# Half differences and sums as two chains with one-bank PSUM tiles, and a bank add on VectorE: a gated mix of two attention branches

## The chip, the cores and the metric

The kernel runs on one core of a Trainium2 chip, in one launch. The metric is the device time of an execution in microseconds (us). TensorE (PE) multiplies matrices, VectorE (DVE), ScalarE (ACT) and GpSimd (POOL) work elementwise, SyncE (SP) issues most transfers. Of these GpSimd reads and writes SBUF only; matmuls land in PSUM, eight banks of 128 x 512 fp32.

## What is computed

Two attention branches on the same input of 2048 positions and 512 features, 32 heads of 16, mixed by a gate for each position (cut to what matters):

```python
g = sigmoid((x * gate_w).sum(-1, keepdims=True))
# A: each position sees itself and 7 earlier ones, 2 apart
qkv = x @ wqkv
logits = einsum("bhsd,bhswd->bhsw", q, kg) * scale      # masked where idx < 0
a = (einsum over w of softmax(logits), vg) @ wo_a
# B: all 2048 positions; 32 query heads share one key head and one value head
scores = einsum("bhqd,bkd->bhqk", x @ wq, x @ wk) * scale
b = (softmax(scores) @ (x @ wv)) @ wo_b
return g * a + (1 - g) * b
```

Branch B needs 32 x 2048 x 2048 scores twice here: once for the maximum over the keys of each query, which is subtracted before the exponential, and once for the exponential itself.

## The kernel before

**Units and steps.** Branch B is cut into 32 units (512 queries by 4 heads). A unit's queries lie stacked in one of eight SBUF tiles (`qst`, the last two of them `q67`), two heads in each 64-row half, so that a matmul over 64 rows runs in one row half of TensorE and another beside it in the other. The attention loop has 512 steps, 16 to a unit (128 keys each): two `exp_pair` (L503; scores of two heads into `eb[0]` or `eb[1]`, two banks each, and ScalarE's exponential of 128 x 1024, L510) and one `weighted` (L515; eight recorded matmuls of the step before into `po`, L518).

**Maxima.** The maximum of a unit must be known before its first step. `slots` lists the work: 1024 entries (unit, pair, 128 queries, 512 keys), two matmuls each, one to a row half. They run ahead of the loop and beside it, in three ways:
- `fill_pair` (L373): two matmuls (`max_mm`, L351) into the two banks of `m2` (`pm` in the profile), and one VectorE maximum over both (L378).
- `fill_one` (L382): one matmul into `m1` (`ps`), or `po` where that is free, and a VectorE maximum (L389). In a loop step it stands alone in its row half.
- the half path, for two key blocks at once, since max(a, b) = (a + b) / 2 + |a - b| / 2. `kcd` holds the half sums and half differences of the keys (`half_keys`, L410). `fill_diff` (L445): two matmuls with the half differences into both banks of `m2` (L443), an Abs by ScalarE on each bank into `dd` (L453). `fill_sum` (L458): a matmul with the half sums into `m1` or `po`, then one VectorE instruction adds `dd` and takes the maximum (L463). Four matmuls as in the plain way, but 2 x 512 columns for VectorE in place of 4 x 512.

Before, one such group of four is open at a time: `pend` holds its two sums, and `fill_diff` runs only when `pend` is empty and both banks of `m2` are free (L783).

**Stages.** First the projection: queries, keys, values of B, then 48 row parts of branch A's projection (`lumps` of kind `a`: three column thirds of 16 row parts), each 12 products split over both row halves (L1124) into `eb`. `a_post` (L260) ends such a part: ScalarE copies both banks out (L274, L275), GpSimd adds them (L281), SP stores. GpSimd then computes branch A's attention in the background (`work`, L1012). The loop is interrupted twice, before step 272 and before step 400, by output phases (`out_phase`, L792; eight and four row blocks of the final projections, L804). The last four output row blocks are spread over the last steps (`spread`, L840, and `spread_some`, L899; L872), once no fills are left, on blocks that `blocks_out` (L711) turns by DMA from step 472 on. If the fills are late, `pause` (L925) stops the loop for them.

**Order.** All instructions are written out by a planner in program order: `clk` estimates the time at which TensorE, ScalarE and VectorE are done, `free` when a PSUM bank can be written again, and work is placed when these say that it is ready. In the projection and the output phases `stream` (L753) does it: it keeps a place in the list of products for each row half, puts a sum or a single in one half and a product in the other, and a pair in a slot of its own. A queue runs in order, so a matmul that must wait holds all behind it. In the loop the main code (L1177 on) asks `fill_ready` (L915) for a pair between the two `exp_pair`, and for a single while `singles` (L911) says that more matmuls are left than the pairs of the remaining steps can take.

## Time and profile before

| what | value |
|---|---|
| median of 3 runs | 1477.92 us (1476.96 to 1478.03) |
| the profiled execution | 1477.72 us, of it the span 1475.9 us |
| granted TensorE clock, mean | 0.997 |
| busy share of the span | PE 99%, DVE 82%, ACT 86%, POOL 69% |
| projection with half groups, 105 to 258 us | ScalarE 127.18 of 153 us, VectorE 104.76 |
| first loop part, from about 258 us | 272 steps |
| first output phase, 836 to 908 us | then 128 steps |
| second output phase, 1175 to 1211 us | then 112 steps |
| tail, 1381 to 1464 us | TensorE 78.97 of 83 us, mean clock 0.96 |

A row of the timeline gives start (us), duration (us), engine, line, operation, written and read tiles, form and count; equal neighbours are merged. Matmuls overlap, so the distance from one start to the next tells more than a duration. In brackets stand the idle time ahead of a row and what ended it. `pe` is `eb`, `pm` is `m2`, `ps` is `m1`, and 62*128 or 64*128 tells rows and columns of the array in use.

### The profile page before, as it was taken

The page shows a single profiled execution, that of the slowest core. Times are in us where ns is not written, and L with a number is a line of the kernel's source. Part 1 is how long each engine was busy: PE and PEld are TensorE (multiplying, and loading weights), DVE is VectorE, ACT ScalarE, POOL GpSimd, SP SyncE. Part 2 cuts the span into 40 slices and gives each one's busy share as a digit, 9 for nine tenths or more (in the row PEclk, how much of TensorE's full clock was granted, in tenths as well). Part 3 has the DMA queues.
Part 4 walks back from the last instruction along what each step waited for, and adds up shares of the span by engine and source line. Part 5 has one row for each costly group of instructions (what it writes and reads, how often), then busy time and mean ns, then how long its engine had stood idle before and what let it go on. Part 6 is the DMA issues. An engine that isn't in the chain of part 4 may idle for free.

```text
span 1475.9 us, 28719 instructions
## 1 busy us (share of the span) xinstructions
PE 1462.1 (99%) x10612; PEld 681.4 (46%) x10612; DVE 1210.2 (82%) x1851; ACT 1269.2 (86%) x1592; POOL 1023.9 (69%) x1772
## 2 busy tenths in 40 slices
PE   9999999999999999999999999999999999999998
PEld 5878787333333333333333475333333363333343
DVE  6976667789898898888898888888888888888922
ACT  5668788999999999999999878999999889999865
POOL 7854988878988989989889898788888231110121
PEclk9999999999999999999999999999999999999999
DMA  6753524121120211211202111121120000000110
GB/s 223 211 161 91 143 72 119 39 85 41 56 70 27 74 60 42 71 40 50 75 7 76 42 67 53 41 71 41 42 70 23 12 31 12 2 1 8 23 30 29
DMA packets 75260, 89.77 MB, mean 61 GB/s; under 512 B 56368, under 2 KB 56416, under 8 KB 70896
## 3 DMA queue, kind: packets, MB, share of 16 engines
q1 hardware_dynamic: 68176, 49.00, 11.7%
q0 software_dynamic: 6368, 37.90, 7.8%
q8 instruction: 83, 1.36, 0.4%
q10 hardware_dynamic: 576, 1.05, 0.2%
q14 instruction: 57, 0.47, 0.1%
HBM read 60.03 MB, written 27.35 MB: 59 GB/s over the span
## 4 chain that ended last, share of the span: by engine, by line
PE 87%; DVE 1%; ACT 1%; SPq 1%; issue 0%; DMA 0%; DVEq 0%; ACTq 0%; POOL 0%
PE po L518 34%; PE pe L508 23%; PE pm L351 8%; PE ps L351 7%; PE pe L1124 5%; PE pe L804 4%; PE pm L443 2%; PE ps L443 1%; PE po L443 1%; PE pm L872 1%; SPq L728 0%; DVE mx L378 0%; PE pe L693 0%; ACT pexp L453 0%; DMA td<-raw 0%
## 5 line engine op out<-in xcount | busy, mean ns | idle before, releaser
L510 ACT ACTIVATE pexp<-pe 128x1024 f32<-128x1024 f32 x1022 | 990.4, 1022 | 105.1 <-PE pe L508 102.1
L378 DVE TENSOR_REDUCE mx<-pm 128x2 f32<-128x1024 f32 x500 | 611.8, 1224 | 117.7 <-PE pm L351 114.8
L518 PE MATMUL po<-pexp,vst 128*32 128x512 f32 x4096 | 546.8, 606 | 0.1
L508 PE MATMUL pe<-qst,kst 64*128 64x512 f32 x1916 | 435.2, 448 | 2.8 <-DVE mx L378 1.8
L508 PEld LDWEIGHTS pe<-qst,kst 64*128 64x128 f32 x1916 | 180.0, 184 | 477.5 <-ACT pexp L510 462.4
L389 DVE TENSOR_REDUCE mx<-ps 128x1 f32<-128x512 f32 x494 | 336.1, 680 | 4.5 <-PE ps L351 4.5
L351 PE MATMUL pm<-kst,qst 62*128 62x512 f32 x942 | 192.2, 396 | 0.9 <-DVE mx L378 0.9
L582 POOL TENSOR_TENSOR pr<-aext 128x256 f32<-128x256 f32 x256 | 182.2, 737 | 0.3
L351 PE MATMUL ps<-kst,qst 62*128 62x512 f32 x459 | 181.9, 396 | 0.4 <-DVE mx L463 0.2
L642 POOL TENSOR_TENSOR oa<-oa,av 128x256 f32<-128x256 f32 x224 | 164.1, 732 | 15.4
L518 PEld LDWEIGHTS po<-pexp,vst 128*32 128x32 f32 x4096 | 80.6, 108 | 180.1 <-issue 171.6
L639 POOL TENSOR_TENSOR av<-aext,lg 128x256 f32<-128x256 f32 x224 | 139.3, 622 | 12.9
L453 ACT ACTIVATE dd<-pm 128x512 f32<-128x512 f32 x150 | 85.0, 609 | 24.3 <-PE pm L443 21.2
L545 POOL TENSOR_TENSOR rl<-rl,gate_t 128x16 f32<-128x16 f32 x31 | 6.9, 222 | 131.0 <-DVE rl L539 97.1
L1124 PE MATMUL pe<-wal,xh 64*128 64x512 f32 x376 | 94.4, 392 | 0.2 <-POOL wal L84 0.2
L1124 PE MATMUL pe<-wah,xh 64*128 64x512 f32 x376 | 93.8, 392 | 0.1
L351 PEld LDWEIGHTS pm<-kst,qst 62*128 62x128 f32 x942 | 92.0, 187 | 3.7 <-DVE mx L378 1.6
L1124 PE MATMUL pe<-wah,xl 64*128 64x512 f32 x376 | 92.9, 392 | 0.0
L463 DVE CUSTOM_DVE_ANT_0 dd<-ps,dd 128x512 f32<-128x512 f32 x75 | 51.9, 692 | 48.3 <-PE ps L443 39.9
L351 PEld LDWEIGHTS ps<-kst,qst 62*128 62x128 f32 x459 | 85.8, 187 | 6.6 <-DVE mx L389 2.4
L588 POOL TENSOR_TENSOR tr<-pr 128x512 f32<-128x512 f32 x64 | 81.7, 1277 | 4.2
L281 POOL TENSOR_TENSOR stage<-stage,two 128x512 f32<-128x512 f32 x48 | 62.5, 1302 | 23.1 <-ACT two L275 22.6
(217 smaller groups left out, 1825.2 us busy)
## 6 DMA issues: line engine op xcount, KB each, us to landing
aext<-ad POOLq DMA_DIRECT2D x32, 1056.0 KB, 5.6
qst<-qd SPq DMA_DIRECT2D x60, 128.0 KB
ad<-stage SPq DMA_DIRECT2D x32, 240.0 KB
xraw<-xt SPq DMA_DIRECT2D x16, 256.0 KB
qd<-qhi SPq DMA_DIRECT2D x16, 256.0 KB
qd<-qlo SPq DMA_DIRECT2D x16, 256.0 KB
qst<-qd SPq DMA_DIRECT2D x60, 64.0 KB
qst<-ml SPq DMA_DIRECT2D x216, 2.0 KB
```

Source lines behind the costliest of these rows:

```text
L351: nc.tensor.matmul(dst, qst[home(v)[0]][b:b + 62, pr, t * P:(t + 1) * P], kst[b:b + 62, kc * 512:(kc + 1) * 512], start=True, stop=True)
L378: nc.vector.tensor_reduce(m[:, :, pr, t, kc], dst, AX.X, ALU.max)
L389: nc.vector.tensor_reduce(m[:, odd, pr, t, kc:kc + 1], dst, AX.X, ALU.max)
L453: nc.scalar.activation(dd[0][:, odd], m2[:, odd, :], AF.Abs)
L508: nc.tensor.matmul(bank[:, odd, :], kst[b:b + 64, kt * P:(kt + 1) * P], qst[home(u)[0]][b:b + 64, pr, :], start=True, stop=True)
L510: nc.scalar.activation(e, bank, AF.Exp, scale=SCALE)
L518: nc.tensor.matmul(po[32 * i:32 * i + 32, :], vst[:, kt, :], pexp[s, i // 2][:, i % 2, :], start=(kt == 0), stop=(kt == NJ - 1))
L582: nc.gpsimd.tensor_mul(pr[:, k], q, e[:, o:o + NH, AC:2 * AC])
L588: nc.gpsimd.tensor_add(nx, cur[:, :, 0:n], cur[:, :, n:2 * n])
L639: nc.gpsimd.tensor_mul(av, e[:, o:o + NH, 2 * AC:].rearrange("p j (h d) -> p j h d", d=DH), lg[:, w].unsqueeze(3).to_broadcast([P, NH, AG, ...
L642: nc.gpsimd.tensor_add(ao, ao, av)
L1124: nc.tensor.matmul(front[2 if x == last else x % 2][0][:, b, :], l[h], r[h], start=(i == 0), stop=(i == 3 * C - 1))
```

## The change

1. **Two chains.** `fill_diff` and `fill_sum` take a row half. `groups` holds groups of which a difference is still to be issued, `pend` the sums that wait, one list for each half, and `half_free` when each bank of `m2` is free. `diff_ready` and `sum_ready` decide for each half, so that in one slot `stream` may place a sum or a difference in one half and a product, or the other half's chain, in the other. `dd` has two buffers in the projection instead of one. At the end of a stream the rest is issued in the same way.
2. **One-bank tiles.** The class `Banks` makes `m2` either one tile of two banks (plain pairs, scores, output rows) or two tiles of one bank each (half path), so that instructions on one bank do not wait for the other's.
3. **Row parts.** For every third row part (j % 3 == 0, but for the first of all; 17 of 48) ScalarE copies one bank only, and VectorE adds the second from PSUM to it. GpSimd's add goes away there.
4. The two tiles that form the half keys' selector share the buffers of tag `aext`.

The core of the diff:

```diff
+class Banks:
+    def shape(self, n):
+        if len(self.tiles) != n:
+            if self.pool:
+                self.pool.release()
+            self.pool = self.tc.alloc_tile_pool(name=self.name + "s", bufs=1, space=PSUM)
+            if n == 1:
+                self.tiles = [self.pool.tile([P, 2, 512], F32, name=self.name)]
+            else:
+                self.tiles = [self.pool.tile([P, 512], F32, name=self.name, tag=f"{self.name}{b}") for b in range(2)]
+        return self
...
-            two = (p2 if j % 3 else pm)[0].tile([P, GN], F32, name="two", tag=("two", "raw", "own")[j % 3], bufs=1)
+            two = p2[0].tile([P, GN], F32, name="two", tag=("", "raw", "own")[j % 3], bufs=1) if j % 3 else None
         own = st[:, j % 2, :]
         nc.scalar.activation(own, bank[:, 0, :], AF.Copy)
-        nc.scalar.activation(two, bank[:, 1, :], AF.Copy)
-        at = after("act", clk["pe"] + T_LAT, 1.05)
+        if two:
+            nc.scalar.activation(two, bank[:, 1, :], AF.Copy)
+        at = after("act", clk["pe"] + T_LAT, 1.05 if two else 0.52)
...
-            nc.gpsimd.tensor_add(own, own, two)
-            pool = max(pool, 1e3 * at) + 1280
+            if two:
+                nc.gpsimd.tensor_add(own, own, two)
+                pool = max(pool, 1e3 * at) + 1280
+            else:
+                nc.vector.tensor_add(own, bank[:, 1, :], own)
+                free[key] = after("dve", at, 0.65) + 0.1
...
-    def fill_diff():
-        v, pr, t, kc = slots.pop(0)
-        slots.pop(0)
-        for odd in range(2):
-            half_mm(m2[:, odd, :], v, pr, t, kc, 1, odd)
...
+    def diff_ready(odd):
+        if max(half_free) != free["m2"]:
+            half_free[:] = [free["m2"]] * 2
+        if half_free[odd] > clk["pe"] or clk["dve"] - 1.6 > clk["pe"]:
+            return False
+        mine = [g for g in groups if odd in g[2]]
+        if not mine and (groups or half or ended or wants or not paired()):
+            return False
+        d = mine[0][1] if mine else dd[0]
+        return all(x[1] is not d for x in pend[odd])
+
+    def fill_diff(odd):
...
+        m2.shape(2)
+        half_mm(m2[:, odd, :], v, pr, t, kc, 1, odd)
+        nc.scalar.activation(d[:, odd], m2[:, odd, :], AF.Abs)
+        half_free[odd] = after("act", clk["pe"] + T_R + T_LAT, 0.54) + 0.1
+        free["m2"] = max(half_free)
+        pend[odd].append(((v, pr, t, kc), d, half_free[odd]))
...
+    def sum_ready(odd):
+        return bool(pend[odd]) and free[("m1", "po")[odd]] <= clk["pe"] + 0.1 and pend[odd][0][2] <= clk["pe"] + 0.4
...
             halves = groups or any(pend) or paired() and not half
             if halves or 1 in wants:
                 for b in range(2):
                     if sum_ready(b):
                         lone[b] = lambda b=b: fill_sum(b)
                     elif diff_ready(b):
                         lone[b] = lambda b=b: fill_diff(b)
                         break
```

Where the program's rows move. First TensorE in the projection, within one of the last row parts (unit 7 of the maxima, `pm` the differences, `ps` and `po` the sums of the two halves). Before:

```order
L443 MATMUL pm<-kcd,qst_82 128x512 x2
L1124 MATMUL pe_85<-wah,xh 128x512 x2
L1124 MATMUL pe_85<-wal,xh 128x512 x2
L443 MATMUL ps<-kcd,qst_82 128x512
L1124 MATMUL pe_85<-wah,xl 128x512 x2
L1124 MATMUL pe_85<-wah,xh 128x512 x2
L1124 MATMUL pe_85<-wal,xh 128x512
L443 MATMUL po<-kcd,qst_82 128x512
L1124 MATMUL pe_85<-wal,xh 128x512
```

In the change, in the same row part:

```order
L480 MATMUL ps<-kcd,q_76 128x512
L1185 MATMUL pe_85<-wal,xh 128x512 x2
L1185 MATMUL pe_85<-wah,xl 128x512
L480 MATMUL pm<-kcd,q_76 128x512
L1185 MATMUL pe_85<-wah,xh 128x512
L480 MATMUL po<-kcd,q_76 128x512
L1185 MATMUL pe_85<-wah,xl 128x512
L480 MATMUL pm<-kcd,q_76 128x512
L1185 MATMUL pe_85<-wah,xh 128x512
```

The pair of differences in a slot of its own has become two single differences, each beside a product or beside the other half's sum, and there are more of them to a row part; over the whole projection 372 half matmuls stand where 300 stood (164 for 140 and 76 for 68 in the output phases).

Second TensorE in the loop at steps 421 and 422 (`ps` the single, L518 or L578 the weighted sum that ends a step). Before:

```order
L508 MATMUL pe_85<-qst_77,kst 128x512 x2
L351 MATMUL pm<-kst,qst_79 128x512 x2
L508 MATMUL pe_86<-qst_77,kst 128x512 x2
L351 MATMUL ps<-kst,qst_79 128x512
L518 MATMUL po<-pexp,vst 32x512 x4
```

In the change, step 421 still with its single and step 422 without:

```order
L384 MATMUL pm<-kst,qst_81 128x512 x2
L568 MATMUL pe_86<-qst_77,kst 128x512 x2
L384 MATMUL ps<-kst,qst_81 128x512
L578 MATMUL po<-pexp,vst 32x512 x4
L568 MATMUL pe_85<-qst_77,kst 128x512 x2
L384 MATMUL pm<-kst,qst_81 128x512 x2
L568 MATMUL pe_86<-qst_77,kst 128x512 x2
L578 MATMUL po<-pexp,vst 32x512 x4
```

From step 422 to 479 the single is gone; before, each step up to 487 has it.

Third TensorE at steps 479 and 480, where in the change the output rows begin (L933). Before, step 480:

```order
L508 MATMUL pe_85<-qst_81,kst 128x512 x2
L351 MATMUL pm<-kst,qst_82 128x512 x2
L508 MATMUL pe_86<-qst_81,kst 128x512 x2
L351 MATMUL ps<-kst,qst_82 128x512
L518 MATMUL po<-pexp,vst 32x512 x4
```

In the change, step 479 and the beginning of step 480:

```order
L384 MATMUL pm<-kst,qst_82 128x512 x2
L568 MATMUL pe_86<-qst_81,kst 128x512 x2
L578 MATMUL po<-pexp,vst 32x512 x4
L568 MATMUL pe_85<-qst_81,kst 128x512 x2
L933 MATMUL pm<-woh_3672,turned_15661 128x512 x6
L568 MATMUL pe_86<-qst_81,kst 128x512 x2
L578 MATMUL po<-pexp,vst 32x512 x4
```

The output rows start at step 480 instead of step 490, and the five pairs on `pe` and `pm` that a pause put ahead of the scores of step 488 are gone.

More of the change, by code (lines that the diff above doesn't have):

```diff
@@ L373, in fill_pair @@
     def fill_pair(dst, key):
+        if dst is m2:
+            dst = m2.whole()
         v, pr, t, kc = slots.pop(0)
@@ L503, in exp_pair @@
     def exp_pair(s, pr, other=False, first=0):
-        bank, key = (m2, "m2") if other else (eb[pr], f"e{pr}")
+        bank, key = (m2.whole(), "m2") if other else (eb[pr], f"e{pr}")
         u, kt = divmod(s, NJ)
@@ L766, in stream @@
+            if halves or 1 in wants:
+                for b in range(2):
+                    if sum_ready(b):
+                        lone[b] = lambda b=b: fill_sum(b)
+                    elif diff_ready(b):
+                        lone[b] = lambda b=b: fill_diff(b)
+                        break
             elif fillable() and free["m1"] <= clk["pe"] + 0.1:
-                single, odd = lambda: fill_one(m1, "m1"), half[0][4] if half else 0
+                lone[half[0][4] if half else 0] = lambda: fill_one(m1, "m1")
@@ L775, in stream @@
                     clk["pe"] = now
                 elif at[b] < len(seq):
[L777 removed]
+                    dur = max(dur, mm(b, seq[at[b]]))
                     at[b] += 1
[L779 to L785 removed]
+            after("pe", 0, T_R if lone else dur)
@@ L786, in stream @@
+            if not (ended or 0 in wants or halves) and slots and fillable() and free["m2"] <= clk["pe"] + 0.1:
                 clk["pe"] = max(clk["pe"], free["m2"])
@@ L831, in out_phase @@
         stream([(x, j, i) for x, j in enumerate(js) for i in range(m)], mm, done, False)
-        while pend:
-            odd = pend[0][4]
-            clk["pe"] = max(clk["pe"], free[("m1", "po")[odd]], ready_d[odd] - 0.3)
-            fill_sum()
+        ended.add(1)
+        while groups or any(pend):
+            for b in range(2):
+                if sum_ready(b):
+                    fill_sum(b)
+                elif diff_ready(b):
+                    fill_diff(b)
             clk["pe"] += T_R
@@ L1163, in gated_mix_kernel @@
     stream([(x, i) for x in range(len(lumps)) for i in range(3 * C)], mm, done_mm, True)
-    assert not pend
+    assert not groups and not any(pend)
     formed.clear()
```

81 lines of the change are left out of this document (43 added, 38 removed).

## Prediction

> **What bounds the kernel now.** I read the page first (span, chain), then busy time by stage, then single steps of the attention loop in order of time, then the tail.
>
> ```profile
> span 1475.9 us, 28719 instructions
> PE 87%; DVE 1%; ACT 1%; SPq 1%; issue 0%; DMA 0%; DVEq 0%; ACTq 0%; POOL 0%
> ```
>
> The chain that ended last is TensorE for 87% of the span. The profiled execution took 1477.72 us (1.8 us outside its span), 0.2 us below the median of 1477.92, so sums against it need no correction. By stage (projection before and from its first half groups on, first output phase, last steps):
>
> ```profile
> core 0: us, PE busy (x) PEld busy (x) DVE busy (x) ACT busy (x) POOL busy (x), PEclk, DMA share, GB/s
> 24.00:105.00 81.00, 79.98 (x641) 64.18 (x641) 70.57 (x99) 51.24 (x109) 64.81 (x57) 1.00 0.63 175
> 105.00:258.00 153.00, 152.38 (x1256) 121.58 (x1256) 104.76 (x310) 127.18 (x255) 117.92 (x161) 1.00 0.41 111
> 836.00:908.00 72.00, 70.99 (x615) 52.41 (x617) 57.80 (x162) 57.41 (x108) 66.33 (x103) 1.00 0.14 49
> 1381.00:1464.00 83.00, 78.97 (x564) 33.16 (x556) 31.23 (x43) 62.23 (x64) 19.23 (x35) 0.96 0.09 20
> ```
>
> TensorE is busy throughout the first three, ScalarE and VectorE are not; only the tail lets TensorE idle, at a mean clock of 0.96. Matmuls over 64 rows run two at a time, one per row half: a slot of the projection takes 153.00 / (1256 / 2) = 0.244 us, of the output phase 72.00 / (615 / 2) = 0.234 us.
>
> A full step of the attention loop (TensorE's rows, then one of ScalarE's):
>
> ```profile
> 500.14 0.50 PE L508 MATMUL pe<-q,kst 64*128 64x512 f32 x2
> 500.48 0.40 PE L351 MATMUL pm<-kst,qst 62*128 62x512 f32 x2
> 500.72 0.39 PE L508 MATMUL pe<-q,kst 64*128 64x512 f32 x2
> 500.95 0.40 PE L351 MATMUL ps<-kst,qst 62*128 62x512 f32 x1
> 501.28 1.07 PE L518 MATMUL po<-pexp,vst 128*32 128x512 f32 x8
> 502.27 0.51 PE L508 MATMUL pe<-q,kst 64*128 64x512 f32 x2
> ```
>
> ```profile
> 502.88 1.94 ACT L510 ACTIVATE pexp<-pe 128x1024 f32<-128x1024 f32 x2 [0.20 <-PE pe L508]
> ```
>
> From 500.14 to 502.27 is 2.13 us: 0.34 + 0.24 + 0.23 + 0.33 + 0.99, with no gap, while ScalarE waits 0.20 us for the next scores. A single maximum matmul (ps) costs a whole slot, 0.23 us, since nothing runs in the other half. So **TensorE's issue order bounds every stage**, and what matters is how many slots the change moves where.
>
> **The change, part by part.** The order says where the 2048 maximum matmuls stand. Half differences and sums: projection 300, now 372 (+72); first output phase 140, now 164 (+24); second 68, now 76 (+8). Plain ones: first loop 790, now 773; middle loop 370 and 372; last loop 271, now 179. So 104 matmuls leave plain fills, mostly of the last loop.
>
> *Projection.* +72 matmuls are 36 slots: 36 x 0.244 = **+8.8 us**, as TensorE has no idle time there that could hide them. Beside it ScalarE gains 36 Abs and loses 17 copies, GpSimd loses 17 adds, VectorE gains 36 reductions and 17 adds:
>
> ```profile
> L453 ACT ACTIVATE dd<-pm 128x512 f32<-128x512 f32 x148 | 83.9, 610 | 23.0 <-PE pm L443 19.9 <-DVE mx L463 2.9
> L463 DVE CUSTOM_DVE_ANT_0 dd<-ps,dd 128x512 f32<-128x512 f32 x74 | 51.2, 692 | 46.4 <-PE ps L443 38.1 <-ACT dd L453 7.2 <-PE pe L1124 0.7
> ```
>
> ```profile
> L747 DVE TENSOR_TENSOR two<-pe,two x12: 685/685/687, 848.6 to 1211.5; 128x512 f32<-128x512 f32 x12
> ```
>
> ScalarE: 83.9 / 148 = 0.57 us of its time per Abs, and a copy of the same shape costs about the same, so (36 - 17) x 0.57 = +10.8 on 127.18, in a window of about 162 us: 138 of 162. VectorE: 36 x 0.69 + 17 x 0.69 = +36.6 on 104.76 (L747 is the same add, bank plus copy): 141 of 162. Neither reaches its limit, so I cost their work at nothing; if that cover fails, TensorE waits (the drains, below). Waits also change: today a difference pair can wait for the Abs of both banks, 49 times in all:
>
> ```profile
>   PEld pm L443: 14.6, 49
> ```
>
> ```profile
> 238.97 0.50 PE L443 MATMUL pm<-kcd,qst 62*128 62x512 f32 x2
> 239.32 0.40 PE L1124 MATMUL pe<-wah,xl 64*128 64x512 f32 x2
> ```
>
> Such a slot took 0.35 us instead of 0.24, so an unmet wait costs **0.11 us** beyond what it waits. Now each bank waits alone, and the planner asks for zero slack where it took 0.1 us; but there are more waits. Bounds: all 49 vanish (-5.4), or as many again (+5.4). I take no change, the nearest count there is. Queued behind a waiting difference stands all of TensorE's stream; behind the new bank add stand VectorE's reductions, 0.69 us of delay each time, which a planner slack of up to 1.6 us covers.
>
> *First loop.* Steps 12 to 18 (seven) have no single and mostly no pair, since more of the eight stacked units are used up; the rest equals before. Before they take 6 x 2.13 + 1.90 (the last step of a unit has no single today either, below) = 14.7 us, now 7 x 2.01 (below) = 14.1: **-0.6**. The unit that the fills wait for comes in by DMA in step 17 and is first used in step 19, by the order; I cost that wait at nothing, as the planner leaves two steps for it.
>
> *Output phases.* (12 + 4) x 0.234 = **+3.7**.
>
> *Steps 422 to 479.* 58 steps lose their single. How fast is such a step? Once per unit there is one today:
>
> ```profile
> 326.09 0.50 PE L508 MATMUL pe<-qst,kst 64*128 64x512 f32 x2
> ...
> 327.99 0.50 PE L508 MATMUL pe<-qst,kst 64*128 64x512 f32 x2
> ...
> 328.71 0.49 PE L508 MATMUL pe<-qst,kst 64*128 64x512 f32 x2
> 329.14 1.06 PE L518 MATMUL po<-pexp,vst 128*32 128x512 f32 x8
> 330.13 0.51 PE L508 MATMUL pe<-qst,kst 64*128 64x512 f32 x2
> ```
>
> ```profile
> 326.72 3.81 ACT L510 ACTIVATE pexp<-pe 128x1024 f32<-128x1024 f32 x4 [0.21 <-PE pe L508]
> 330.74 1.02 ACT L510 ACTIVATE pexp<-pe 128x1024 f32<-128x1024 f32 x1 [0.21 <-PE pe L508]
> ```
>
> The step from 326.09 took 1.90 us, but in the next one ScalarE ran four exponentials back to back ((3.81 - 1.02) / 3 = 0.93 apart), and the second scores (328.71) waited for the end of the second (326.72 + 0.93 + 1.02 = 328.67). What is late next is this ring over two steps: scores to weighted sum 0.43, to next scores 0.99, to their exponential 0.61, to the second 0.93, its run 1.02, release 0.04 = 4.02 us, **2.01 us a step**. Bounds: TensorE's 1.90 below, today's 2.13 above. 58 x (2.13 - 2.01) = **-7.0** (-13.3 to 0).
>
> *Tail, steps 480 to 510.* Before:
>
> ```profile
> 1380.59 1.06 PE L518 MATMUL po<-pexp,vst 128*32 128x512 f32 x8
> ...
> 1400.80 0.51 PE L351 MATMUL pe<-kst,qst 62*128 62x512 f32 x2 [0.93 <-DVE mx L378]
> 1401.93 0.50 PE L351 MATMUL pm<-kst,qst 62*128 62x512 f32 x2 [0.62 <-DVE mx L378]
> 1404.19 1.22 PE L508 MATMUL pe<-qst,kst 64*128 64x512 f32 x4 [1.76 <-DVE mx L378]
> ...
> 1444.42 0.51 PE L508 MATMUL pe<-qst,kst 64*128 64x512 f32 x2
> ...
> 1446.78 0.51 PE L508 MATMUL pe<-qst,kst 64*128 64x512 f32 x2
> ...
> 1462.51 1.07 PE L518 MATMUL po<-pexp,vst 128*32 128x512 f32 x8
> ```
>
> From 1380.59 to 1462.51, 31 steps, are 81.9 us: fills until step 487, a pause that ends the last fills (three waits for VectorE, then half clock), then the last four output rows at three to five pairs a step, 2.36 us with three. Now the fills are over at step 479, and the same 84 row pairs spread over 480 to 510: by the order eleven steps with three pairs, twenty with two (2.36 - 0.23 = 2.13): 11 x 2.36 + 20 x 2.13 = 68.6. At each of three row changes VectorE empties the bank in two passes; I allow 0.2 us each, an estimate: 69.2, **-12.7**. Bounds: -14, or -5 if the rows wait for their inputs.
>
> By the Trainium skill ("TensorE: Matmul & The Clock Gate", Part 1) the clock halves after an idle window of some 3.4 us; the 0.96 in the tail's row agrees. By that rule a new wait of such length anywhere would cost another stretch at half clock: the sum would be 1473 (the tail's row has 83.00 x 0.04 = 3.3 us of clock lost), against 1470 without.
>
> Sum: +8.8 - 0.6 + 3.7 - 7.0 - 12.7 = -7.8; 1477.7 - 7.8 = **1470 us**.
>
> At nothing as well: the selector matrices move into buffers of the bank copies, whose third add comes before them on GpSimd, and the pair bank changes its shape between stages, where its last reader was waited for already. That the change doesn't do what it says is no rival: the order rows shown with it have its moves.
>
> **The rivals.**
> - *The drains bound the projection* (slower). In the first output phase, where the same chains run, VectorE was 57.80 / 72.00 = 80% busy and ScalarE 80% too, and the rest went in waits for each other and TensorE. If the projection's chains reach no more than that, VectorE's 141.4 us need 177 us, not 162: 1470 + 15 = 1485, seen as unmet waits of 0.11 us and more before half matmuls. It decides from 82% on (141.4 / (161.8 + 10.8)). For: VectorE goes from 68% to 87%, and 612 half matmuls now wait one by one. Against: in the projection's first part (24 to 105 us) VectorE held 87% with TensorE 99% busy. A rule speaks for it: the Trainium skill, "TensorEngine Tiling (Array Packing)", PSUM Bottleneck, says that tiling speeds up TensorE but not the emptying of PSUM, which may then become the bottleneck. By the rule the sum ends at 1485, by the row from 24 to 105 us at 1470; no row has these chains at 87%.
> - *TensorE's own 1.90 for the steps without a single* (58 x 0.11 = 6 more) *and half of the 49 waits gone* (2 to 3 more): 1462. Against: ScalarE's ring above.
> - *The rows wait.* They start ten steps earlier, on blocks turned by DMA from step 472 on; if these are late, the tail gains 5, not 12.7: 1478.
>
> **How the numbers follow.** Forecast 1470 (1465 to 1474, the bounds of the waits): 0.60. Drains, 1485: 0.17. Faster still, 1462: 0.13. Late rows, 1478: 0.10. A measurement of this kernel can tell 0.2%, 3 us. Faster by more than that (under 1475): 0.60 + 0.13 less 0.02 for the forecast's upper edge = 0.71; same: 0.10 + 0.02 = 0.12; slower: 0.17. A range to 1482 leaves out most of the drains' case and little else: 1462 to 1482.
>
> **What would show it.** Right: the loop starts about 9 us later; steps 422 to 479 at 2.01; no pause at step 488 and a clock of 1.00 there; first weighted sum of step 480 to that of 510 about 69 us. Wrong: difference matmuls of 0.50 us in the projection by the hundred, or a wait for blocks in the first steps of the tail.

## The result, and the profile after

The changed kernel takes **1475.81 us** (median of 20 runs, 1475.48 to 1476.37) against 1478.03 of the kernel before in the same session: a ratio of **0.9984, 95% interval [0.9977, 0.9991]**. It is 2.2 us faster, where 1470, 7.8 us faster, was forecast. The direction was right, the size was not: less than a third of the gain arrived.

The page of the changed kernel, span and chain of waits:

```profile
span 1474.1 us, 29007 instructions
PE 97%; DVE 1%; ACT 1%; issue 1%; POOL 0%; DMA 0%; DVEq 0%; SPq 0%; ACTq 0%; POOLq 0%
```

TensorE carries 97% of the chain now, and the tail no longer idles. Busy time by stage (projection in two parts, first output phase, steps 476 to 510):

```profile
core 0: us, PE busy (x) PEld busy (x) DVE busy (x) ACT busy (x) POOL busy (x), PEclk, DMA share, GB/s
24.00:105.00 81.00, 79.62 (x637) 64.86 (x636) 71.88 (x104) 50.80 (x109) 63.03 (x55) 1.00 0.63 174
105.00:270.00 165.00, 162.90 (x1335) 122.18 (x1333) 137.23 (x398) 139.88 (x279) 118.95 (x193) 1.00 0.38 105
848.00:922.00 74.00, 73.53 (x623) 52.22 (x619) 63.04 (x185) 61.79 (x118) 66.24 (x105) 1.00 0.17 57
1382.00:1462.00 80.00, 80.00 (x600) 31.68 (x598) 15.97 (x26) 70.94 (x74) 19.33 (x35) 1.00 0.11 23
```

The last row has TensorE busy for all of its 80 us at a clock of 1.00 (0.96 before), as forecast. In the projection VectorE is at 137.23 of 165 us, 83%, and ScalarE at 85%: close to the loads that were worked out, and still not full.

The first matmuls of the weighted sums (L578) of steps 0, 479 and 510 give the stages; step 480 begins behind the second of them:

```profile
272.45 0.64 PE L578 MATMUL po<-pexp,vst 128*32 128x512 f32 x4
...
1391.95 1.06 PE L578 MATMUL po<-pexp,vst 128*32 128x512 f32 x8
...
1460.85 1.06 PE L578 MATMUL po<-pexp,vst 128*32 128x512 f32 x8
```

| stage (start of one step's weighted sum to another's) | before | after | difference | forecast |
|---|---|---|---|---|
| projection, to step 0 | 260.62 | 272.45 | +11.8 | +8.8 |
| steps 0 to 18 | 38.99 | 37.57 | -1.4 | -0.6 |
| step 19 | 2.13 | 3.21 | +1.1 | 0 |
| first output phase (with its step) | 70.28 | 75.51 | +5.2 | +2.8 |
| second output phase | 35.71 | 37.22 | +1.5 | +0.9 |
| steps 401 and 402 | 4.49 | 5.16 | +0.7 | 0 |
| steps 422 to 479 | 123.94 | 116.67 | -7.3 | -7.0 |
| steps 480 to 510 | 81.92 | 68.90 | -13.0 | -12.7 |
| everything else | | | -0.5 | 0 |

The two large gains came within 0.3 us of the forecast. The costs did not: the stages with half matmuls took 6 us more than forecast, and single places another 1.8.

**Slots or waits?** A slot is a pair of matmuls that start together, one per row half. Counting slots between the first and the last of a stage, and taking 0.229 us for each, what is left over is time in which a slot was late:

| | slots before | left over | slots after | left over |
|---|---|---|---|---|
| projection | 967 | 14.6 us | 1003 | 18.2 us |
| first output phase | 272 | 6.0 us | 286 | 8.0 us |
| second output phase | 135 | 2.8 us | 141 | 3.0 us |

So 56 slots more, 12.8 us, where the forecast had 52 and 12.5 us; and 5.8 us more of late slots (29.2 us in place of 23.4), where it had none.

**Which slots are late.** Here is one sum in the projection of the changed kernel, on TensorE, with the one before it in the same bank (ps):

```profile
174.95 0.40 PE L480 MATMUL ps<-kcd,qst 62*128 62x512 f32 x1
...
175.90 0.39 PE L1185 MATMUL pe<-wal,xh 64*128 64x512 f32 x1
176.25 0.49 PE L480 MATMUL ps<-kcd,qst 62*128 62x512 f32 x1
...
176.60 0.39 PE L1185 MATMUL pe<-wah,xh 64*128 64x512 f32 x1
```

The weight load of the second sum, and VectorE's reduction of the first between the two:

```profile
176.25 0.18 PEld L480 LDWEIGHTS ps<-kcd,qst 62*128 62x128 f32 x1 [0.39 <-DVE mx L523]
```

```profile
175.50 0.69 DVE L523 CUSTOM_DVE_ANT_0 dd<-ps,dd 128x512 f32<-128x512 f32 x1
176.12 0.08 DVE L523 DVE_READ_ACCUMULATOR2_ANT mx<- 128x1 f32 x1
```

The sum stands five slots behind the one before it in its bank, 5 x 0.23 = 1.15 us. But the ring takes longer: matmul start to reduction 0.55, reduction 0.69 and 0.01, then 0.05 to the next matmul: 1.30 us. VectorE was not late here; it began 0.55 us behind the matmul, about as early as it ever does (over all sums of the projection, the reduction ends 1.22 us behind the matmul at best, and the next matmul of that bank starts at 1.29). So the slot ahead of the sum lasts 0.35 us instead of 0.23, and the slot behind it 0.35 as well.

The planner (L516 and L524) thinks the ring is 0.23 + 0.20 + 0.66 + 0.08 = 1.17 us and lets a sum go 0.1 us before that, at 1.07: five slots pass, and five slots are too short. In the changed kernel 38 sums of the projection, 23 of the first output phase and 11 of the second stand five slots (one of them four) behind the last in their bank; the slots next to these 72 are 12.2 us longer than 0.229 each. In the kernel before, whose one group had to finish before the next began, none of the projection's sums stands closer than six; in the output phases four do.

Two more losses are single events. On GpSimd a weight split (L112) waits behind another split and an add, and TensorE for it; and in step 19 a fill waits for unit 8's DMA:

```profile
205.76 1.29 POOL L112 TENSOR_TENSOR wal<-waraw,wah 128x512 fp32r<-128x512 f32 x1
207.00 1.30 POOL L311 TENSOR_TENSOR stage<-stage,two 128x512 f32<-128x512 f32 x1
208.25 1.27 POOL L112 TENSOR_TENSOR wal<-waraw,wah 128x512 fp32r<-128x512 f32 x1
```

```profile
209.58 0.49 PE L1185 MATMUL pe<-wal,xh 64*128 64x512 f32 x1 [1.50 <-POOL wal L112]
```

```profile
312.56 0.47 PE L384 MATMUL pm<-kst,qst 62*128 62x512 f32 x1 [0.80 <-DMA qst<-qd]
```

### The profile page after: what moved, and what is told of

Same layout as the page of the kernel before. It is cut to its first block, busy times and chain, and to the rows that moved or that the text cites. A ratio compares the mean times of both kernels' runs of the same rounds, so it can differ in the third digit from the quotient of the medians.

```text
span 1474.1 us, 29007 instructions
## 1 busy us (share of the span) xinstructions
PE 1461.2 (99%) x10612; PEld 670.5 (45%) x10612; DVE 1191.0 (81%) x1880; ACT 1289.0 (87%) x1629; POOL 1001.4 (68%) x1753
## 4 chain that ended last, share of the span: by engine, by line
PE 97%; DVE 1%; ACT 1%; issue 1%; POOL 0%; DMA 0%; DVEq 0%; SPq 0%; ACTq 0%; POOLq 0%
PE po L578 34%; PE pe L568 23%; PE pe L1185 11%; PE pm L384 8%; PE ps L384 7%; PE pe L862 5%; PE pm L480 3%; PE po L480 2%; PE ps L480 2%; PE pm L933 1%; PE pe L208 1%; ACT pexp L570 1%; DVE qst L186 0%; POOL wal L112 0%; PE pe L753 0%
## 5 line engine op out<-in xcount | busy, mean ns | idle before, releaser
L413 DVE TENSOR_REDUCE mx<-pm 128x2 f32<-128x1024 f32 x491 | 600.9, 1224 | 147.2 <-PE pm L384 136.4
L578 PE MATMUL po<-pexp,vst 128*32 128x512 f32 x4096 | 545.5, 605 | 0.0
L424 DVE TENSOR_REDUCE mx<-ps 128x1 f32<-128x512 f32 x420 | 285.7, 680 | 0.0
L384 PE MATMUL ps<-kst,qst 62*128 62x512 f32 x408 | 161.4, 396 | 0.3 <-DVE mx L424 0.2
L578 PEld LDWEIGHTS po<-pexp,vst 128*32 128x32 f32 x4096 | 80.5, 108 | 171.3 <-issue 162.6
L506 ACT ACTIVATE dd<-pm 128x512 f32<-128x512 f32 x186 | 104.9, 604 | 23.4 <-PE pm L480 13.1
L1185 PE MATMUL pe<-wal,xh 64*128 64x512 f32 x376 | 118.8, 395 | 1.9 <-POOL wal L112 1.9
L1185 PE MATMUL pe<-wah,xh 64*128 64x512 f32 x376 | 119.8, 397 | 0.0
L1185 PE MATMUL pe<-wah,xl 64*128 64x512 f32 x376 | 118.9, 395 | 0.0
L506 ACT ACTIVATE pexp<-pm 128x512 f32<-128x512 f32 x120 | 68.2, 603 | 13.7 <-PE pm L480 9.5
L384 PEld LDWEIGHTS ps<-kst,qst 62*128 62x128 f32 x408 | 76.1, 187 | 6.4 <-DVE mx L424 3.4
L648 POOL TENSOR_TENSOR tr<-tr 128x256 f32<-128x256 f32 (+1 forms) x128 | 72.4, 565 | 8.8
```

What stands on the lines that cost most here:

```text
L384: nc.tensor.matmul(dst, qst[home(v)[0]][b:b + 62, pr, t * P:(t + 1) * P], kst[b:b + 62, kc * 512:(kc + 1) * 512], start=True, stop=True)
L413: nc.vector.tensor_reduce(m[:, :, pr, t, kc], dst, AX.X, ALU.max)
L424: nc.vector.tensor_reduce(m[:, odd, pr, t, kc:kc + 1], dst, AX.X, ALU.max)
L506: nc.scalar.activation(d[:, odd], m2[:, odd, :], AF.Abs)
L578: nc.tensor.matmul(po[32 * i:32 * i + 32, :], vst[:, kt, :], pexp[s, i // 2][:, i % 2, :], start=(kt == 0), stop=(kt == NJ - 1))
L648: nc.gpsimd.tensor_add(nx, cur[:, :, 0:n], cur[:, :, n:2 * n])
```

## The experiments

The theory: the half matmuls of the chains come earlier than their banks can be free, because the planner's clock is too fast for the ring through VectorE, and each costs a late slot or two. The rivals: half matmuls cost more than half a slot by themselves, since slots stay half empty; or VectorE (or ScalarE) has no capacity left. All kernels below are the changed one with the edit shown; medians are to be read beside its 1475.81, ratios are to the kernel before, run on the same chip (1478.3 to 1478.6).

**1. Drains made short, TensorE's order kept.**

```diff
-nc.scalar.activation(d[:, odd], m2[:, odd, :], AF.Abs)
+nc.scalar.activation(d[:, odd, 0:64], m2[:, odd, 0:64], AF.Abs)
-nc.vector.tensor_tensor_reduce(d[:, odd], dst, d[:, odd], 1.0, -FMAX, ALU.add, ALU.max, m[:, odd, pr, t, kc:kc + 1])
+nc.vector.tensor_tensor_reduce(d[:, odd, 0:64], dst[:, 0:64], d[:, odd, 0:64], 1.0, -FMAX, ALU.add, ALU.max, m[:, odd, pr, t, kc:kc + 1])
```

> The Abs on ScalarE and the fused reduction on VectorE that empty the banks of the half matmuls work on 64 of the 512 columns, in the projection and in both output phases; TensorE's order is that of the changed kernel, row for row. The output's shifts are then maxima over fewer keys. Theory of waits (half matmuls wait for the drain of their bank, or work queued behind the drains comes late): in the projection the time above 0.229 us a slot, 18.9 us now, falls by 6 to 8 (all slots longer than 0.25 us before or behind a half matmul), in the output phases, 11.2 us now, by 3 to 5, so the kernel takes 1464 to 1467 us. Rival of slots (the matmuls of the two row halves no longer start together, half slots stay empty, drains have no part in it): at most the late weight split goes, 1.7 us, so 1474 to 1476 us.

Measured 1462.81 us, 0.9894 [0.9881, 0.9908]. The loop starts 7.8 us earlier, the output phases are 4.5 and 1.7 us shorter, and the rest is about 0.5 us longer:

```profile
264.61 0.64 PE L578 MATMUL po<-pexp,vst 128*32 128x512 f32 x4
```

The order of matmuls is the same, so slots stay what they are, and the rival of half-empty slots is out: **14.1 us of the changed kernel are waits for the drains**, in the output phases more than the theory allowed for (the weight split is still late here, 1.9 us at 202.2). Left over above 0.229 for each of the same slots are 10.3, 3.5 and 1.3 us, 15.1 in all. The kernel before has 23.4, so part of that may be waits for drains too; its drains were not shortened in any run.

**2. Only VectorE's reduction short.**

```diff
-nc.vector.tensor_tensor_reduce(d[:, odd], dst, d[:, odd], 1.0, -FMAX, ALU.add, ALU.max, m[:, odd, pr, t, kc:kc + 1])
+nc.vector.tensor_tensor_reduce(d[:, odd, 0:64], dst[:, 0:64], d[:, odd, 0:64], 1.0, -FMAX, ALU.add, ALU.max, m[:, odd, pr, t, kc:kc + 1])
```

> Only VectorE's fused reduction is shortened to 64 of 512 columns (it leaves 448 columns out of the maxima); the Abs on ScalarE stays whole, TensorE's order stays. Theory of waits, VectorE's part: in the projection of the changed kernel 68 of 79 waits of half matmuls' weight loads end with VectorE, 11 with ScalarE; so most of the gain of the run with both drains short comes here: 4 to 5 us in the projection and 2 in the output phases, 1468 to 1470 us. Rival (ScalarE's Abs is what the chain waits for, the reduction only waits behind it): under 1.5 us, 1474 to 1476 us.

Measured 1465.80 us, 0.9915 [0.9901, 0.9928]: 5.6, 4.1 and 1.6 us in the three stages, 11.3 of the 14.1 us of run 1. That is more than was expected (1468 to 1470 us): it is mainly VectorE's side of the chain. This does not yet tell load from distance: the edit took away both.

**3. The last weight split on VectorE.**

```diff
-    def split_wa(gg, c):
+    def split_wa(gg, c, eng=nc.gpsimd):
-split(wah[gg, c], wal[gg, c], waraw.pop((gg, c)), nc.gpsimd)
+split(wah[gg, c], wal[gg, c], waraw.pop((gg, c)), eng)
-split_wa(lump[1] + 1, c)
+split_wa(lump[1] + 1, c, nc.vector if c == C - 1 else nc.gpsimd)
```

> Only the last weight split of the second and third column group runs on VectorE instead of GpSimd; TensorE's and ScalarE's orders stay row for row. Theory: the 1.67 us pause of TensorE at 207.67 us and the part of the slot at 141.7 us above its length (0.5 us) are a split that came late on GpSimd behind an add; they go, the loop starts 1.5 to 2.2 us earlier, 1473.6 to 1474.3 us. Rival (VectorE, 83% busy there, has no room: each split of 0.69 us delays the reductions and TensorE waits for these instead): the loop starts within 0.5 us of where it does now, 1475 to 1476 us.

Measured 1475.23 us, 0.9978 [0.9969, 0.9987]. The loop starts 1.4 us earlier, so the pause was the split's; but step 19 grew by 0.33 us, as unit 8's load went out only 1.2 us earlier (306.74 us), and steps 401 and 402 by 0.23. The whole gained 0.6 us, less than forecast: one wait's time went partly into the next.

**4. Unit 7's DMAs behind unit 8's load.**

```diff
-            if pe:
+            if pe and v != NB - 1:
                 shift_d(v, ml, k)
```

> The eight small DMAs that bring unit 7's maxima into its queries, which stand on SP's queue ahead of the loads of unit 8, are issued behind these; no engine's order of instructions changes but SP's. Theory: the 1.1 us that step 19 takes longer than before is the wait for unit 8's load, which SP could only issue at 308 us because the eight DMAs ahead of it waited for unit 7's maxima until 302.65 us and took 5.2 us; step 19 falls from 3.21 to 2.13 us, 1474.7 us. Rival (the transfer is slow, since a 1 MB load of the other branch runs at the same time, and the queue has no part in it): step 19 stays above 2.8 us, 1475.4 to 1476 us.

Measured 1474.80 us, 0.9974 [0.9965, 0.9984]; step 19 takes 2.13 us. SP's queue in the changed kernel, then in this one:

```profile
302.65 5.21 SPq L556 DMA_DIRECT2D q<-ml  x8
307.96 0.62 SPq L353 DMA_DIRECT2D qst<-qd  x1
```

```profile
301.77 0.61 SPq L353 DMA_DIRECT2D qst<-qd  x1
...
306.46 7.29 SPq L556 DMA_DIRECT2D q<-ml  x8
```

Eight DMAs of 2 KB stood ahead of unit 8's load; they waited for unit 7's maxima and then took 5.2 us to issue. Behind them the load went out at 308 us, while the planner counts it as there 5 us after its step. Without them it goes out 6 us earlier. In the kernel before the load stood ahead of the eight (it went out at 291.0 us, they from 300.5 on). The queue was the cause, not the transfer.

**5. VectorE's bank add short.**

```diff
-nc.vector.tensor_add(own, bank[:, 1, :], own)
+nc.vector.tensor_add(own[:, 0:64], bank[:, 1, 0:64], own[:, 0:64])
```

> VectorE's add of the second bank of every third row part works on 64 of 512 columns (448 columns of these parts lack the second half of their sum); TensorE's order stays row for row. Theory (the added 0.69 us each stand in VectorE's queue ahead of reductions for which half matmuls wait): 17 adds, each of them delaying a reduction by some tenths of a us, and the loop starts 2 to 3 us earlier, 1473 to 1474 us. Rival (the planner counts the add and keeps the half matmuls away from it, the waits come from its general lack of slack): under 0.7 us, 1475 to 1476 us.

Measured 1476.30 us, 0.9984 [0.9975, 0.9993]. The loop starts 0.6 us earlier and nothing is gained in all. The rival holds: the added VectorE work is not what the half matmuls wait for.

**6. 0.1 us of slack for every half matmul.**

```diff
-if half_free[odd] > clk["pe"] or clk["dve"] - 1.6 > clk["pe"]:
+if half_free[odd] > clk["pe"] - 0.1 or clk["dve"] - 1.6 > clk["pe"]:
-return bool(pend[odd]) and free[("m1", "po")[odd]] <= clk["pe"] + 0.1 and pend[odd][0][2] <= clk["pe"] + 0.4
+return bool(pend[odd]) and free[("m1", "po")[odd]] <= clk["pe"] - 0.1 and pend[odd][0][2] <= clk["pe"] + 0.4
```

> The planner issues a half matmul only when its bank has been free for 0.1 us by its own clock, where it took a bank up to 0.1 us before (sums) or just when free (differences). By the order the half matmuls become 344 in the projection (from 372), 136 and 72 in the output phases (from 164 and 76), and the fills still end at step 479. Theory (the waits come from that lack of slack): 30 slots fewer, -6.9 us, waits -4 to -6, and 60 maxima back in steps 422 to 479 as single matmuls at 0.12 us, +7.2: 1470 to 1472.5 us, with the projection at 264 to 266 us. Rival (VectorE has no capacity left for its reductions, and waits stay whatever the slack): waits per half matmul as now, the slots alone against the singles, 1475.5 to 1476.5 us.

Measured 1466.97 us, **0.9917 [0.9903, 0.9931]**, better than the theory had it. The loop starts at 266.5, the output phases take 68.0 and 36.0 us (75.5 and 37.2), steps 422 to 479 give 5.6 back for their singles. Two sums in all are left at five slots. The projection still has a pause of 1.9 us, which VectorE's add of a row part's second bank (L314) ends and in which the clock fell (last section):

```profile
206.19 0.76 PE L1185 MATMUL pe<-wah,xh 64*128 64x512 f32 x1 [1.52 <-DVE stage L314]
```

So a bank add can stop TensorE; in the changed kernel itself the profile shows no wait of TensorE for any of the 17.

**7. 0.4 us of slack.**

```diff
-if half_free[odd] > clk["pe"] or clk["dve"] - 1.6 > clk["pe"]:
+if half_free[odd] > clk["pe"] - 0.4 or clk["dve"] - 1.6 > clk["pe"]:
-return bool(pend[odd]) and free[("m1", "po")[odd]] <= clk["pe"] + 0.1 and pend[odd][0][2] <= clk["pe"] + 0.4
+return bool(pend[odd]) and free[("m1", "po")[odd]] <= clk["pe"] - 0.4 and pend[odd][0][2] <= clk["pe"] + 0.4
```

> The same with 0.4 us: 300 half matmuls in the projection, the number of before, 120 and 60 in the output phases (140 and 68 before); the fills end at step 489 (487 before). Theory of waits: with the number of before the chains lose the waits that the pairs of before had too, so the loop starts 3 to 6 us earlier than before's 260.6, at 255 to 258 us, and the output phases are 3 to 5 us shorter than before's 70.3 and 35.7 together; the longer tail costs 2 to 5: 1469 to 1474 us. Rival (half matmuls cost what they cost, waits follow VectorE's load): the loop starts where it did before, within 1 us, and the time is 1477 to 1479 us.

Measured 1484.12 us, 1.0034 [1.0021, 1.0046]. The loop starts at 257.3 us, 3.3 earlier than before with the same 300 half matmuls, and the output phases take 102.4 us together, 3.6 less than before: this part went by the theory. The tail did not. Two steps took 11.2 us each, one of them here:

```profile
1358.57 0.50 PE L384 MATMUL pe<-kst,qst 62*128 62x512 f32 x2 [0.18 <-DVE mx L424]
1359.70 0.50 PE L384 MATMUL pe<-kst,qst 62*128 62x512 f32 x2 [0.64 <-DVE mx L413]
1360.84 0.80 PE L384 MATMUL pm<-kst,qst 62*128 62x512 f32 x2 [0.63 <-DVE mx L413]
1361.97 0.79 PE L384 MATMUL pe<-kst,qst 62*128 62x512 f32 x2 [0.33 <-DVE mx L413]
1365.36 0.79 PE L568 MATMUL pe<-qst,kst 64*128 64x512 f32 x2 [2.60 <-DVE mx L413]
```

A unit was due whose maxima were not complete, and the loop stood still for fills that wait for VectorE one by one (as in the tail of before, at step 488); the last rows take 0.79 us instead of 0.50: the clock was halved (0.53 on average from 1366 to 1371 us). 28 maxima more in the loops than before cost 14 us there: the price of a maximum is 0.12 us as a single, and far more once it misses its unit's start. My sum for this run had only the first price.

**8. Edits 3 and 4 together.**

```diff
-split_wa(lump[1] + 1, c)
+split_wa(lump[1] + 1, c, nc.vector if c == C - 1 else nc.gpsimd)
-            if pe:
+            if pe and v != NB - 1:
                 shift_d(v, ml, k)
```

> The last weight split on VectorE and unit 7's DMAs behind unit 8's loads, both at once: the two single events among the losses. By the two runs apart (1.38 us in the projection, of which step 19's wait took 0.33 back; 1.08 us at step 19) 2.5 us: 1473.1 to 1473.6 us. If instead the one is again covered by the other's wait: 1474 us or more.

Measured 1473.92 us, 0.9966 [0.9953, 0.9978]: 1.9 us, where 2.5 was expected and the two alone gained 0.6 and 1.0 in all.

**9. Only the tolerance of the sums taken out.**

```diff
-return bool(pend[odd]) and free[("m1", "po")[odd]] <= clk["pe"] + 0.1 and pend[odd][0][2] <= clk["pe"] + 0.4
+return bool(pend[odd]) and free[("m1", "po")[odd]] <= clk["pe"] and pend[odd][0][2] <= clk["pe"] + 0.4
```

> One tolerance of the planner is taken out: a sum may be issued when its bank is free by the planner's clock, no longer 0.1 us before. By the order the half matmuls stay 372 in the projection, 164 and 76 in the output phases, the fills end at step 479. Theory of the ring: from a sum's matmul to the end of its reduction the trace of the changed kernel has 1.22 us at least, to the next matmul in the same bank 1.29; the planner takes 1.17 and lets a sum go at 1.07, so it sets sums five slots (1.15 us) apart, 38 in the projection, 23 and 11 in the output phases, and the slots at and behind these 72 sums are 12.2 us longer than 0.229 each. Without the tolerance they stand six slots (1.38 us) apart: 9 to 12 us less, the loop starts at 266 to 268 us, the output phases take 71 to 72 and 35 to 36 us: 1464 to 1467 us. Rival (VectorE as a whole is too busy, the waits move to other half matmuls): 1472 to 1475 us.

Measured 1468.53 us, **0.9933 [0.9921, 0.9946]**: 7.3 us from one constant, with as many half matmuls in each stage as before the edit. Two sums of one bank at their closest in the projection, now six slots apart:

```profile
152.30 0.40 PE L480 MATMUL ps<-kcd,qst 62*128 62x512 f32 x1
...
153.46 0.40 PE L1185 MATMUL pe<-wal,xh 64*128 64x512 f32 x2
153.69 0.40 PE L480 MATMUL ps<-kcd,qst 62*128 62x512 f32 x1
...
153.94 0.41 PE L480 MATMUL pm<-kcd,qst 62*128 62x512 f32 x1
```

The second sum comes 1.39 us behind the first, and the slots around it take 0.23 and 0.25 us. VectorE has no less to do. Here is the projection from 105 us to just before step 0's weighted sum, in the changed kernel and then without the tolerance:

```profile
105.00:272.00 167.00, 164.90 (x1351) 123.51 (x1347) 137.23 (x398) 141.52 (x281) 120.79 (x196) 1.00 0.38 105
```

```profile
105.00:268.00 163.00, 160.74 (x1351) 122.84 (x1347) 136.88 (x398) 141.64 (x281) 120.98 (x197) 1.00 0.39 108
```

The same 398 instructions of VectorE, 137 us of work, fit into 163 us as into 167 (84% busy, 82% before the edit). TensorE's weight loads for sums wait 13.3 us in all for VectorE in place of 16.9, and no sum of the projection is left at five slots: **the cause is the distance between sums, not VectorE's capacity**. The projection gained 4.1 us of the 5.6 counted at its sums, the output phases 1.9 of 6.6, where ten sums still come too early; step 19 lost its wait by the by (2.13 us). So the forecast was too large by a third: some of the time at these sums is taken up by whatever comes late next.

**10. The tolerance out, with edits 3 and 4.**

```diff
-return bool(pend[odd]) and free[("m1", "po")[odd]] <= clk["pe"] + 0.1 and pend[odd][0][2] <= clk["pe"] + 0.4
+return bool(pend[odd]) and free[("m1", "po")[odd]] <= clk["pe"] and pend[odd][0][2] <= clk["pe"] + 0.4
-split_wa(lump[1] + 1, c)
+split_wa(lump[1] + 1, c, nc.vector if c == C - 1 else nc.gpsimd)
-            if pe:
+            if pe and v != NB - 1:
                 shift_d(v, ml, k)
```

> The run without the tolerance, with the last weight split on VectorE and unit 7's DMAs behind unit 8's loads added. If the late split and the queue are losses of their own, 1.5 to 2.5 us less than without the two. Rival (with the sums in time VectorE is where it must be and the split pushes it out of step again, or the loop's start at another time leaves step 19 no wait): within 0.7 us of the run without them.

Measured 1468.37 us, 0.9932 [0.9919, 0.9944]: as run 9. The rival holds; with step 19 already free of its wait, edit 4 had nothing to gain. Edit 3 took away the late split's wait, but the loop starts no earlier (268.6 us, 268.3 in run 9): the time went into other slots.

**11. VectorE's adds undone, GpSimd adds all row parts.**

```diff
-two = p2[0].tile([P, GN], F32, name="two", tag=("", "raw", "own")[j % 3], bufs=1) if j % 3 else None
+two = p2[0].tile([P, GN], F32, name="two", tag=("raw", "own")[j % 2], bufs=1)
```

> The bank adds on VectorE are undone: ScalarE copies both banks of every row part and GpSimd adds them, as before the change; the chains stay. By the order the half matmuls are 352, 144 and 84 (from 372, 164 and 76). Theory of the ring (the sums' distance is what costs, the adds on VectorE do not): 32 fewer half matmuls are 16 slots, -3.7 us, and 32 more singles in the loop at 0.12, +3.8; the sums five slots apart stay: 1474 to 1477 us. Rival (VectorE's adds are the overload): the waits of half matmuls shrink by half or more, 1468 to 1471 us.

Measured 1473.76 us, 0.9970 [0.9958, 0.9981]. 76 sums stay at five slots and lose 13.4 us beside them. The waits did not halve, so the adds are not the overload; the 2.1 us gained are a little more than the theory had.

**12. The tolerance out and VectorE's adds undone.**

```diff
-return bool(pend[odd]) and free[("m1", "po")[odd]] <= clk["pe"] + 0.1 and pend[odd][0][2] <= clk["pe"] + 0.4
+return bool(pend[odd]) and free[("m1", "po")[odd]] <= clk["pe"] and pend[odd][0][2] <= clk["pe"] + 0.4
-two = p2[0].tile([P, GN], F32, name="two", tag=("", "raw", "own")[j % 3], bufs=1) if j % 3 else None
+two = p2[0].tile([P, GN], F32, name="two", tag=("raw", "own")[j % 2], bufs=1)
```

> Without the tolerance and without the bank adds on VectorE: 352, 148 and 76 half matmuls. Theory of the ring: what the adds on VectorE buy is 36 half matmuls at half a slot each (4.1 us) against as many singles in the loop (4.3): within 1.5 us of the run that only lacks the tolerance, 1463 to 1468 us. Rival (the adds on VectorE stand in the chains' way): 2 us or more below that run.

Measured 1470.49 us, 0.9949 [0.9936, 0.9963], 2.0 us slower than run 9. That is against the rival, and also outside the theory's 1.5 us. By the medians the adds on VectorE pay about 2 us when the sums come in time and cost about 2 when they don't (run 11); the intervals of the ratios overlap in both pairs, so this is a hint and no more.

**13. The tolerance out in the projection, slack 0.1 in the output phases.**

```diff
-if half_free[odd] > clk["pe"] or clk["dve"] - 1.6 > clk["pe"]:
+if half_free[odd] > clk["pe"] - (0.1 if p2b else 0.0) or clk["dve"] - 1.6 > clk["pe"]:
-return bool(pend[odd]) and free[("m1", "po")[odd]] <= clk["pe"] + 0.1 and pend[odd][0][2] <= clk["pe"] + 0.4
+return bool(pend[odd]) and free[("m1", "po")[odd]] <= clk["pe"] - (0.1 if p2b else 0.0) and pend[odd][0][2] <= clk["pe"] + 0.4
```

> In the projection only the tolerance of the sums is taken out (0.1 us to 0), in the output phases sums and differences both get 0.1 us of slack. By the order 372, 140 and 68 half matmuls, the fills end at step 479. Theory (the waits in the output phases, 5.4 us above 0.229 a slot with the tolerance out and 1.8 us with the slack, belong to the half matmuls' lack of slack there): first output phase 68 to 69 us, second 35.3 to 36.2, the loop starts at 268.3; 32 singles come back at 0.12 us: 1465 to 1467 us. Rival (the short output phase of the run with slack everywhere came from what the projection had left to fill, not from the slack): first output phase above 71 us, 1469 us or more.

Measured **1465.78 us, 0.9916 [0.9902, 0.9929]**, the fastest median of all versions that do the whole work (run 6's ratio lies within its interval): the loop starts at 268.0 us, the output phases take 68.6 and 34.9 us, as the theory had it.

**14. Slack for the differences alone.**

```diff
-if half_free[odd] > clk["pe"] or clk["dve"] - 1.6 > clk["pe"]:
+if half_free[odd] > clk["pe"] - 0.1 or clk["dve"] - 1.6 > clk["pe"]:
```

> Only the differences get 0.1 us of slack, the sums keep their tolerance. By the order 348, 148 and 60 half matmuls (372, 164, 76). Theory of the ring (sums five slots apart are the cost): they stay, each of them with 0.17 us, and 56 half matmuls fewer (28 slots, -6.4 us) stand against 56 more singles (+6.7): 1472 to 1476 us. Rival (the wait of the differences for the Abs is the cost and the sums only follow): 1466 to 1469 us.

Measured 1469.98 us, 0.9942 [0.9930, 0.9955], between the two. Differences that come later make sums that stand further apart: 21 of them are left at five slots, not 72. So this run does not separate the Abs from the sums, and how much each is worth stays open. Run 9, which leaves the differences alone, shows 7.3 us for the sums.

## Why the prediction was wrong, step by step

- *+72 half matmuls are 36 slots, +8.8.* Right: 36 slots by count (8.2 us at 0.229 us each; the 0.244 of the forecast holds some waiting).
- *"I take no change"* for unmet waits, with bounds of 5.4 us either way. **This is the step that failed**: late slots grew by 5.8 us over projection and output phases, a little more than even the upper bound. The bound was made from the 49 waits that the old pairs showed, at 0.11 us each. But the old pairs waited for ScalarE, and the new chains' sums wait for VectorE; the count of the old waits could not bound the new. What the trace of before did hold was the ring: its sums' reductions also end 1.22 us behind the matmul, and the planner's numbers for it stand in the code. Set side by side, 1.22 against 1.07 would have shown that sums could come too early, and the order would have told how many stand at five slots. By count the two bounds came true together: the slots next to the 72 close sums hold 12.2 us (0.17 us a sum, not 0.11), and all other late slots fell from about 23 us to 17, so much of the old pairs' waiting did go.
- *Planner slack "of up to 1.6 us covers" the bank adds.* Right for the changed kernel: shortening them gained nothing (run 5). With other places for the half matmuls one add did stop TensorE (run 6).
- *The rival of the drains* had the right place and the wrong reason and price. It asked whether VectorE's load fits, and put 15 us on it; the load fits (84% busy in run 9), the latency between two sums does not. The Trainium skill ("TensorEngine Tiling (Array Packing)", PSUM Bottleneck) says that copying out of PSUM may become the bottleneck after tiling has made TensorE 4 times faster; here two row halves are enough for 14.1 us to hang on it (run 1). But run 9 gains 7.3 us, 6.0 of them in the same stages, by the distance alone, with VectorE's work unchanged: that part is latency, not throughput.
- *The weight split* is not in the prediction, which has GpSimd lighter by 17 adds. One split came late, 1.4 us of the projection (run 3).
- *First loop: the wait of step 19 "at nothing, as the planner leaves two steps for it".* Wrong by 1.1 us: eight small DMAs ahead on SP's queue, which I had not followed (run 4).
- *Output phases, 16 slots.* By count 20, four of them half empty or out of step: +0.9 us. The rest of the excess is the same wait as above.
- *Steps 422 to 479 at 2.01 us.* Right: 116.67 / 58 = 2.01. ScalarE's two-step ring held, and the rival with TensorE's 1.90 is out.
- *Tail, 69 us, no pause, clock 1.00.* Right: 68.9, so the rival of late rows is out too.
- *Steps 401 and 402, +0.7 us:* not foreseen. In step 401 TensorE waits for ScalarE's exponentials:

```profile
1230.83 0.50 PE L568 MATMUL pe<-qst,kst 64*128 64x512 f32 x2 [0.15 <-ACT pexp L570]
1231.74 0.50 PE L384 MATMUL pm<-kst,qst 62*128 62x512 f32 x2 [0.42 <-ACT pexp L570]
```

  It is not the drains of the sums: with these short (run 1) step 401 takes 3.07 us, against 3.04. In run 9 most of it is gone (4.62 us for both steps, 4.49 before). What makes the exponentials late was not tried alone.

Together: 5.8 (late slots) + 1.1 (step 19) + 0.7 (steps 401 and 402) + 0.3 (slots) - 1.9 (steps 0 to 18 and the other stages a little better than forecast) is the 6 us between -7.8 and the -1.8 of the two spans.

## What to carry to other kernels

When a change lets two chains run where one ran, don't bound its new waits by counting the old ones: work out the ring of each bank (matmul, latency, drain, release) from the trace and hold it against the distance, in slots, at which the order sets two users of the bank. A planner constant that is 0.2 us too short is harmless until a chain is dense enough to hit it, and then it costs two late slots each time. And the busy share of an engine, 82% or 84% here, does not tell whether others wait for it: look at the distance between two users of a bank.

## What the runs showed of the hardware

- **A late weight load lengthens two slots.** Where the sum at 176.25 us had to wait for its weights (rows above), the slot ahead and the slot behind lasted 0.35 us each instead of 0.23. At the 38 close sums of the projection the slots ahead lost 3.0 us and the slots behind 2.6, so they lasted 0.31 and 0.30 us on average.
- **The clock can halve without a long pause.** In run 6 no matmul started between 204.3 and 206.2 us (1.52 us idle), and the row behind it reads:

```profile
206.20:209.00 2.80, 2.80 (x14) 2.44 (x16) 0.81 (x4) 1.59 (x4) 2.49 (x5) 0.50 0.61 157
```

  TensorE's clock is 0.50 for 2.8 us, 14 matmuls where full clock would do about 24. The changed kernel's pause of 1.9 us from 207.69 us on (1.50 us idle) had no such sequel:

```profile
209.57:212.00 2.43, 2.42 (x19) 1.95 (x21) 1.47 (x5) 1.43 (x3) 2.19 (x5) 1.00 0.79 200
```

  Run 6 had two shorter waits in the 2.5 us ahead of its pause. In run 7 short waits were enough: its matmuls go from 0.50 to 0.80 us at 1360.84 us, behind waits of 0.18, 0.64 and 0.63 us (rows there; the mean clock is 0.72 from 1356 to 1366 us). In the tail of the kernel before, the half clock came with waits of 0.93, 0.62 and 1.76 us (rows in the prediction). So several waits close together seem to count, and not only the longest; this is read from four places and was not tried. The Trainium skill ("TensorE: Matmul & The Clock Gate", Part 1) puts the idle window at some 3.4 us. No single wait in these places was as long, so the 0.96 of the tail, which the prediction took for agreement, does not bear that rule out.
